# Filling the key and query stacks by way of DRAM, in a fused attention and gated-feed-forward kernel

## The chip, the cores and the metric

The kernel runs on one core of a Trainium2 chip. A core has five engines that run their own instruction streams: PE multiplies matrices (its weight loads, PEld, overlap the multiplications), DVE and ACT work element by element, POOL does the masks, and SP does nothing here but issue transfers (DMAs), in program order. The transfers are carried by 16 DMA engines, which all transfers share. The metric is the time of one execution on the device in microseconds (us), lower is better. Before the change the median of three runs is 737.2 us (735.12 to 738.53).

## The reference

One input `x` of 2048 tokens by 512 features goes through two branches, and a gate mixes them:

```python
qkv = x @ wqkv                      # 32 heads of 16
scores = einsum("bhqd,bhkd->bhqk", q, k) * 16 ** -0.5
mask = (i - j >= 0) & (i - j < 256) # each query sees itself and the 255 keys before it
a = (softmax(where(mask, scores, -1e9)) @ v) @ wo
b = (sigmoid(x @ w_gate) * (x @ w_up)) @ w_down    # 1376 hidden features
g = sigmoid((x * gate_w).sum(-1, keepdims=True))
out = g * a + (1 - g) * b
```

All inputs are fp32, and so is the result.

## The kernel before, in words

Precision: a product of two fp32 matrices is made as three products of split operands (high by high, high by low, low by high). A high part is a rounded copy made on ACT, the low part is the difference, made on DVE.

Attention: the 32 heads are taken in 8 groups of 4, a group's 2048 tokens in 16 blocks of 128. That makes 128 blocks `u` (NU); the main loop runs over them. For each block PE computes scores in both orientations: `s_part` (L324) gives queries by keys, of which DVE takes the row maximum (L330); `st_part` (L372), nine blocks later (LAG), gives keys by queries, of which ACT takes the exponential (L377). POOL masks the exponentials, and every fourth block `pv_part` (L407) multiplies them with the values. Between these pieces PE does the projections of later groups (`pj`, L252) and the gate and up products of the feed-forward branch (`gu`, L252); the list of turns is fixed in the program, and every engine but POOL keeps the written order. After the last block comes the down product (`pd`) and the output projection (`pa`).

Stacks: `s_part` and `st_part` do not read queries and keys as they were projected but as a *stack* of high and low parts, so that one multiplication over 64 rows gives the split product. A stack `t` holds 8 blocks (two projections `s`, 2t and 2t+1, of 512 columns each), and three of them lie in a ring (`ring`, RING = 3), so stack t takes the place of stack t-3. There are 16. The ring tile has 128 rows. In every group of four rows the rows 1, 2 and 3 hold feature values (high, low, high for keys or queries as the case may be), and row 0 is for constants and maxima. The path of a projection into the ring is: ACT copies it out of the accumulator (`pr`, L264); later ACT makes the high part `sh` (L275) and DVE the low part `sl` (L279), both 128 rows by 1024 columns once both halves are there; `stack_build` then issues one transfer that fills a constant row and twelve transfers of 32 rows by 4 KB that spread 32 rows of `sh` or `sl` over every fourth row of the ring (8 from `sh`, 4 from `sl`). They are issued from block u = 8t-7 on, four per block (SD); the stack is first read at block 8t.

Maxima: the softmax subtracts the row maximum inside the multiplication: the maximum of each query is a row of the stack. Every fourth block, the *visit*, `max_split` (DVE, L340 to L345) makes the negated maxima `nt` of four blocks; `max_store` (L348) writes them to DRAM (`max_scratch`), and `max_load` (L355, two transfers) reads them into row 0 of every 32 rows of the ring. `max_load` waits for its `max_store` to have landed. In a visit SP issues, in this order: `max_store`; four stores of the attention output `oT_scratch<-ob` and one of its sums (they wait for ACT's copy of the pv accumulator); `max_load`; and, in every second visit, the first stack transfers. `st_part` reads what `max_load` brought two blocks after the visit (where a visit opens a new group of heads, four blocks after).

Other traffic on SP: results of `gu` go to DRAM (`gu_scratch<-sp`), new weights come in (`guraw`, `wqraw`), and near the end four raw pieces of the last feed-forward columns (`tailraw`). The latter share two buffers with other weights; piece 2 can be loaded only after piece 0 has been split (`tail_split`, ACT then DVE, L534 and L535). `TAIL_LOAD` and `TAIL_SPLIT` give the block of each.

Each transfer signals one of eight semaphores in turn, and waits for the one eight places before it on SP.

Of the kernel before, what the change touches and what calls it, by code (L numbers as in the profile page):

```python
# [7 lines left out]
F32 = mybir.dt.float32  # L8
# [28 lines left out]
RING = 3  # L37
CH2 = 2 * CH
LAG = 9
PVLAG = LAG + 4  # L40
SD = 4
QB = 32
HOLD = 3
GAPS = [3] * 12 + [2] * 3
SHIFT = 6
TURN = ((0, 2, 1), (1, 0, 2))
TAIL_LOAD = {109: 0, 111: 1, 113: 2, 114: 3}
TAIL_SPLIT = {111: 0, 113: 1, 116: 2, 117: 3}
TREAD = 133
WD_LOAD = {124: 0, 125: 1, 126: 2, 127: 3, 128: 4, 129: 5, 130: 6, 131: 7, 132: 8, 133: 9, 135: 10}  # L50
WO = 125
# [6 lines left out]
def gated_mix_kernel(  # L58
# [11 lines left out]
    nc = tc.nc  # L70
# [22 lines left out]
    gu_d = nc.dram_tensor("gu_scratch", (2, NFM, P, T), F32, kind="Internal").ap()  # L93
    tail_d = nc.dram_tensor("tail_scratch", (NB, P, 2 * TF), F32, kind="Internal").ap()
    max_d = nc.dram_tensor("max_scratch", (NG * NC, P // QB, HG, 2, 4, QB), F32, kind="Internal").ap()
    fill_d = nc.dram_tensor("fill_scratch", (2, CH2), F32, kind="Internal").ap()

    cpool = ctx.enter_context(tc.tile_pool(name="cpool", bufs=1))
# [2 lines left out]
    ring = [ring_t[:, :, r * CH2:(r + 1) * CH2] for r in range(RING)]  # L101
# [34 lines left out]
    with ExitStack() as actx:  # L136
# [107 lines left out]
        pj = {}  # L244
        raws = {}
        parts = {}
        stg = {}

        def group_mm(pt, wh, wl, c, k, half, second):
            d, w = divmod(k, 2) if k < 2 * ND else (k - 2 * ND, 2)  # L250
            r = slice(0, P) if half is None else slice(64 * half, 64 * half + 64)
            return mm(pt, (wl if w == 2 else wh)[r, d], (xl if w == 1 else xh)[r, d, c * CH:(c + 1) * CH],  # L252
                      start=k == 0 and not second, stop=k == 3 * ND - 1 and (half is None or second),
                      skip_group_check=half is not None)
# [22 lines left out]
        def proj_lo(s):  # L277
            sh, sl = parts.pop(s)
            nc.vector.tensor_tensor(sl, pj.pop(s), sh.bitcast(F32), op=ALU.subtract)  # L279

        def stack_build(t):
            assert not {2 * t, 2 * t + 1} & {*pj, *parts}
            sh, sl = (v.bitcast(F32) for v in stg.pop(t))
            rt = ring[t % RING].bitcast(F32)
            st = rt.rearrange("(a r) j f -> r a j f", r=4)
            dmas = [fill_rows(t % RING, 0, 0)]
            if t < RING:
                dmas.append(fill_rows(t, 1, 1))
            for low in range(2):
                for j in range(4):  # L290
                    for r in range(3):
                        if low == (r == (1 if j < 2 else 2)):
                            dmas.append((st[r + 1, :, j], (sl if low else sh)[32 * j:32 * j + 32]))
            return dmas

        def run_dmas(dmas):
            for dst, src in dmas:
                nc.sync.dma_start(dst, src)  # L298
# [51 lines left out]
        def max_load(s):  # L350
            st = ring[s // 2 % RING].bitcast(F32).rearrange("(a r) j f -> r a j f", r=QB)
            o = s % 2 * CH
            src = max_d[s].rearrange("a (p s) l b t -> p (s l) b a t", p=2)
            for p in range(2):
                nc.sync.dma_start(  # L355
                    st[0, :, p, o:o + CH].rearrange("r (b a t) -> r b a t", b=4, a=P // QB), src[p],
                )
# [33 lines left out]
                    compare_op=ALU.is_gt, fill=0.0, base=0, channel_multiplier=1,  # L391
                )

        later = []
        acts = []
        evac = []
        exps = []
# [121 lines left out]
        def tail_load(d):  # L519
            raw_gu[d] = cpool.tile([P, D], F32, tag="wqraw", name=f"tailraw{d}", bufs=2)  # L520
            nc.sync.dma_start(raw_gu[d][:, 0:TW], wgu_tail[d])
# [97 lines left out]
        held = []  # L619

        def proj_group(s):
            return lambda k, h=None, x=False: proj_mm(s, k, h, x), lambda: None, lambda: proj_out(s)
# [148 lines left out]
        sdma = []  # L771
# [6 lines left out]
        for u in range(N):  # L778
# [9 lines left out]
                load_gu(0, 0)  # L788
                load_gu(0, 1)
            if u % 8 == 1 and u > 8 and u // 8 + 1 < NP:  # L790
                sdma = stack_build(u // 8 + 1)
            if u % 16 == 8 and u // 16 + 2 < NG:
                raw_q = load_wqk(u // 16 + 2)
            if u in (4, 8, NU):
# [25 lines left out]
            for s4 in proj_at.get(u, ()):  # L820
# [2 lines left out]
                        lambda k, h, s4=s4: proj_slot(s4, k, h), lambda s4=s4: proj_sum(s4)))  # L823
                else:
                    work.append(proj_group(s4))
            while held and u >= 8 * (held[0][0] // 2) - 10:
                acts.append(held.pop(0)[1])
            if u == N - 1:
                hold_group(*rest.pop(0))
# [74 lines left out]
        def blocks(v):  # L904
            return v.rearrange("p (d t) -> p d t", d=ND)
# [9 lines left out]
        rows = [blocks(free_slot(0, k, 3)) for k in range(2)]  # L915
# [32 lines left out]
        for n, (c, f) in enumerate(steps):  # L948
# [45 lines left out]
            for t in range(4):  # L994
                r = slice(t * QB, (t + 1) * QB)
# [67 lines left out]
```

## Time and profile before

| what | value |
|---|---|
| median of three runs | 737.2 us (735.12 to 738.53) |
| the profiled execution | 737.48 us, its span from first to last instruction 735.8 us |
| granted PE clock | 0.999 |
| busy share: PE, PEld, DVE, ACT, POOL | 99%, 80%, 66%, 58%, 23% |
| bytes moved by DMA | 103.64 MB, mean 141 GB/s |

How to read it: a row of the timeline gives the start in us, the length in us, the engine (SPq is SP issuing, not moving), the line, the operation, what is written and read, the shapes and a count; idle time before it and what ended it stand in brackets. A DMA's row on SPq is the time SP took to issue it; it lands later. A view by windows gives busy time per engine, the granted clock, the mean busy share of the 16 DMA engines, and GB/s. The view of DMA packets counts what the DMA engines carried in a window: each packet is one run of bytes, and the small packets include the 4-byte writes by which each DMA engine that took part in a transfer tells that its share has landed. A busy PE is not PE at its peak, since matmuls are pipelined and their ends are modelled.

### The profile page before, as it was taken

How to read it: one execution, taken by the hardware profiler on the slowest of the kernel's cores; microseconds unless marked ns; L12 is line 12 of the kernel's file. 1: busy time of each engine (PE TensorE's matmuls, PEld its weight loads, DVE VectorE, ACT ScalarE, POOL GpSimd, SP SyncE). 2: the span in 40 equal slices, each digit the busy share in tenths (PEclk: the TensorE clock that was granted, in tenths of full speed). 3: DMA queues.
4: the chain of work that ended last, by engine and by line, in shares of the span. 5: the costliest groups of instructions: out<-in, count | busy, mean ns of one | idle time of the engine just before them, and what ended most of it. 6: DMA issues, size and time to landing. Idle time of an engine off the chain costs nothing.

```text
span 735.8 us, 17513 instructions
## 1 busy us (share of the span) xinstructions
PE 724.9 (99%) x6298; PEld 591.0 (80%) x6298; DVE 488.4 (66%) x1455; ACT 423.5 (58%) x890; POOL 167.0 (23%) x255
## 2 busy tenths in 40 slices
PE   9999999999999999999999999999999999999997
PEld 7888788778887788787888777878888888888886
DVE  5368767666776676766677676666846787658481
ACT  6423666566676566656667655765667564534341
POOL 5200333232233233323223322232332000000000
PEclk9999999999999999999999999999999999999999
DMA  8441425344253442534525335362667997779431
GB/s 288 120 116 41 107 81 157 96 129 133 89 165 87 153 134 74 158 99 132 146 86 144 108 100 136 100 187 94 195 185 209 239 258 197 204 162 262 125 80 58
DMA packets 97039, 103.64 MB, mean 141 GB/s; under 512 B 47646, under 2 KB 60446, under 8 KB 96952
## 3 DMA queue, kind: packets, MB, share of 16 engines
q1 hardware_dynamic: 96808, 102.39, 49.8%
q8 instruction: 50, 0.82, 0.5%
q14 instruction: 37, 0.30, 0.1%
q10 hardware_dynamic: 144, 0.13, 0.1%
HBM read 45.32 MB, written 31.99 MB: 105 GB/s over the span
## 4 chain that ended last, share of the span: by engine, by line
PE 93%; DMA 2%; SPq 2%; issue 1%; DVE 1%; ACT 1%; DVEq 0%; ACTq 0%
PE gu L252 26%; PE pv L407 11%; PE pj L252 10%; PE s L324 6%; PE st L372 5%; PE tp L542 5%; PE pd L87 5%; PE pd L86 5%; PE pd L88 5%; PE vh L579 3%; PE pa L86 2%; PE pa L88 2%; PE pa L87 2%; SPq L298 2%; PE vps L445 2%
## 5 line engine op out<-in xcount | busy, mean ns | idle before, releaser
L330 DVE CUSTOM_DVE_ANT_0 junk<-s,mask 128x384 f32<-128x384 f32 (+2 forms) x512 | 272.0, 531 | 143.1 <-PE s L324 75.3
L377 ACT ACTIVATE pbuf<-st 128x384 f32<-128x384 f32 (+2 forms) x512 | 241.3, 477 | 166.6 <-PE st L372 110.7
L252 PE MATMUL gu<-xh,w 64*128 64x512 f32 x1152 | 282.4, 393 | 0.0
L252 PE MATMUL gu<-xl,w 64*128 64x512 f32 x576 | 186.8, 391 | 0.0
L372 PE MATMUL st<-ring 64*128 64x384 f32 (+2 forms) x536 | 167.7, 329 | 4.1 <-DMA ring<-max_scratch 2.8
L383 POOL TENSOR_SCALAR_AFFINE_SELECT pbuf<-pbuf 128x512 f32<-128x512 f32 x128 | 83.9, 655 | 376.0 <-ACT pbuf L377 334.9
L252 PEld LDWEIGHTS gu<-xh,w 64*128 64x128 f32 x1152 | 156.9, 185 | 11.6
L324 PE MATMUL s<-ring 64*128 64x384 f32 (+2 forms) x536 | 164.5, 325 | 1.0 <-DVE mx L330 0.6
L324 PEld LDWEIGHTS s<-ring 64*128 64x128 f32 x536 | 94.9, 184 | 22.5 <-DVE mx L330 7.2
L372 PEld LDWEIGHTS st<-ring 64*128 64x128 f32 x536 | 96.1, 184 | 11.9 <-ACT pbuf L377 2.3
L252 PEld LDWEIGHTS gu<-xl,w 64*128 64x128 f32 x576 | 90.5, 185 | 3.7
L407 PE MATMUL pv<-pbuf,V 128*32 128x384 f32 (+2 forms) x1408 | 84.3, 386 | 0.0
L252 PE MATMUL pj<-xl,wqh 64*128 64x512 f32 (+1 forms) x228 | 83.1, 392 | 0.0
L252 PE MATMUL pj<-xh,wqh 64*128 64x512 f32 (+1 forms) x228 | 83.0, 393 | 0.0
L407 PEld LDWEIGHTS pv<-pbuf,V 128*32 128x32 f32 x1408 | 41.4, 110 | 40.9 <-issue 30.5
L389 POOL TENSOR_SCALAR_AFFINE_SELECT pbuf<-pbuf 128x512 f32<-128x512 f32 x112 | 73.8, 659 | 0.0
L252 PE MATMUL pj<-xh,wql 64*128 64x512 f32 (+1 forms) x228 | 70.5, 393 | 0.0
L86 PE MATMUL pd<-ring,hb 128*128 128x512 f32 x160 | 62.3, 389 | 0.0
L88 PE MATMUL pd<-ring,hb 128*128 128x512 f32 x160 | 62.3, 389 | 0.0
L87 PE MATMUL pd<-ring,hb 128*128 128x512 f32 x160 | 62.2, 389 | 0.0
L82 ACT CAST hb<-V 128x512 fp32r<-128x512 f32 x40 | 24.9, 622 | 57.9 <-DVE V L743 44.8
L504 ACT COPY sp<-gu 128x512 f32<-128x512 f32 x72 | 42.2, 586 | 3.9 <-DMA gu_scratch<-sp 3.9
(127 smaller groups left out, 1108.9 us busy)
## 6 DMA issues: line engine op xcount, KB each, us to landing
gu_scratch<-sp SPq DMA_DIRECT2D x72, 256.0 KB
V<-gu_scratch SPq DMA_DIRECT2D x36, 512.0 KB
ring<-sh SPq DMA_DIRECT2D x128, 128.0 KB
ring<-sl SPq DMA_DIRECT2D x64, 128.0 KB
guraw<-in_wgu_dram SPq DMA_DIRECT2D x18, 256.0 KB
oT_scratch<-ob SPq DMA_DIRECT2D x128, 32.0 KB
xl<-oT_scratch SPq DMA_DIRECT2D x16, 256.0 KB
V<-in_xT_dram SPq DMA_DIRECT2D x15, 256.0 KB
```

Of the source, the lines that this page charges most:

```text
L86: mm(ps, lh, rh, start=first, stop=False)
L87: mm(ps, lh, rl, start=False, stop=False)
L88: mm(ps, ll, rh, start=False, stop=last)
L252: return mm(pt, (wl if w == 2 else wh)[r, d], (xl if w == 1 else xh)[r, d, c * CH:(c + 1) * CH], start=k == 0 and not second, stop=k == 3 ...
L324: mm(pt[:, (k - k0) * P:(e - k0) * P], lhsT, blk(g, k, hh, 1, e - k), start=k == k0, stop=e == i + 1, skip_group_check=True,)
L330: nc.vector.tensor_tensor_reduce(junk[:, 0:n], pt[:, 0:n], mask[:, 3 * P - n:], scale=1.0, scalar=NEG, op0=ALU.add, op1=ALU.max, accum_out ...
L372: mm(pt[:, (q - j) * P:(e - j) * P], lhsT, blk(g, q, hh, 0, e - q), start=q == j, stop=e == last, skip_group_check=True,)
L377: exps.append(nc.scalar.activation(p_blk(u, hh, 0, n), pt[:, 0:n * P].rearrange("p (b t) -> p b t", t=P), AF.Exp, scale=SCALE,))
L383: nc.gpsimd.affine_select(pbuf[:, s0], pbuf[:, s0], pattern=[[0, HG], [1, P]], compare_op=ALU.is_ge, fill=0.0, base=0, channel_multiplier=-1,)
L389: nc.gpsimd.affine_select(old, old, pattern=[[0, HG], [-1, P]], compare_op=ALU.is_gt, fill=0.0, base=0, channel_multiplier=1,)
L407: mm(pv[32 * hh:32 * hh + 32, (q - q0) * P:(e - q0) * P], Vf[:, v:v + 32], p_blk(g * NB + j, hh, q - j, e - q), start=j == j0, stop=j == q ...
L504: nc.scalar.copy(t, gp.pop((f, c, w)))
```

## The change

`sh` and `sl` of a stack are no longer spread from on-chip memory into the ring. As soon as the second half of `sl` is made, two stores (512 KB each) write them to a DRAM scratch of 4 by 2 by 32 by 1024 values per ring place; from block 8t-7 on, where the twelve transfers stood, five loads read them back into the ring (one of 512 KB, four of 256 KB), after the constant row's transfer, three per block (SD = 3). Stacks 0 and 1 are made as before; 14 are changed. To have the parts earlier, the making of `sh` and `sl` may begin at block 8t-13 instead of 8t-10. Two of the tail's raw pieces are loaded one block later, one a block earlier, and the first two are split earlier.

```diff
-SD = 4
+SD = 3
-TAIL_LOAD = {109: 0, 111: 1, 113: 2, 114: 3}
-TAIL_SPLIT = {111: 0, 113: 1, 116: 2, 117: 3}
+TAIL_LOAD = {109: 0, 110: 1, 114: 2, 115: 3}
+TAIL_SPLIT = {110: 0, 111: 1, 116: 2, 117: 3}
...
+    stack_d = nc.dram_tensor("stack_scratch", (RING, 4, 2, QB, CH2), F32, kind="Internal").ap()
...
         def proj_lo(s):
             sh, sl = parts.pop(s)
             nc.vector.tensor_tensor(sl, pj.pop(s), sh.bitcast(F32), op=ALU.subtract)
+            t = s // 2
+            made[t] = made.get(t, 0) + 1
+            if t > 1 and made[t] == 2:
+                for low, v in enumerate(stg.pop(t)):
+                    later.append((stack_d[t % RING, :, low], v.bitcast(F32)))
+
+        def stack_load(t):
+            assert made[t] == 2
+            rows = ring[t % RING].bitcast(F32).rearrange("(a r) j f -> r a j f", r=4)
+            dmas = [fill_rows(t % RING, 0, 0)]
+            if t < RING:
+                dmas.append(fill_rows(t, 1, 1))
+            for r, low, js in ((0, 0, (0, 4)), (1, 1, (0, 2)), (1, 0, (2, 4)), (2, 0, (0, 2)), (2, 1, (2, 4))):
+                js = slice(*js)
+                dmas.append((rows[r + 1, :, js], stack_d[t % RING, js, low].rearrange("j a f -> a j f")))
+            return dmas
...
             if u % 8 == 1 and u > 8 and u // 8 + 1 < NP:
-                sdma = stack_build(u // 8 + 1)
+                sdma = stack_load(u // 8 + 1)
...
-            while held and u >= 8 * (held[0][0] // 2) - 10:
+            while held and u >= 8 * (held[0][0] // 2) - 13:
                 acts.append(held.pop(0)[1])
```

PE's instructions keep their order entirely, and so do POOL's. On ACT and DVE only the makings of `sh` and `sl`, the splits beside them and the tail's first split move. SP's order changes at every stack. In the rows below, a shape stands behind each transfer (of what it writes), a count behind that, and an added list names the semaphores it waits for; after the change the program's line numbers are 17 higher there.

The first place is SP at stack 4, blocks 22 to 25. Before:

```order
121 L151 DMA wqraw_1850<-in_wqk_dram 128x512 [waits DMAHW1_49]
122 L298 DMA gu_scratch<-sp_3_1_1796 128x512 [waits DMAHW2_49,Activation_49]
123 L348 DMA max_scratch<-nt_1926 128x32 [waits DMAHW3_49,DVE_49]
124 L298 DMA oT_scratch<-ob_1937 16x512 [waits DMAHW4_49,Activation_49]
125 L298 DMA oT_scratch<-ob_1937 16x512 [waits DMAHW5_49]
126 L298 DMA oT_scratch<-ob_1937 16x512 [waits DMAHW6_49]
127 L298 DMA oT_scratch<-ob_1937 16x512 [waits DMAHW7_49]
128 L298 DMA sum_scratch<-ob_1937 4x512 [waits DMAHW0_49]
129 L355 DMA ring<-max_scratch 4x16x32 [waits DMAHW3_49,DMAHW1_49,PE_49]
130 L355 DMA ring<-max_scratch 4x16x32 [waits DMAHW2_49,PE_49]
131 L298 DMA ring<-fill_scratch 4x2x1024 [waits PE_49]
132 L298 DMA ring<-sh_1747 32x1024 [waits DMAHW4_49]
```

And now:

```order
111 L316 DMA gu_scratch<-sp_3_1_1786 128x512 [waits DMAHW0_49,Activation_49]
112 L316 DMA stack_scratch<-sh_1539 4x32x1024 [waits DMAHW1_49,Activation_49]
113 L316 DMA stack_scratch<-sl_1540 4x32x1024 [waits DMAHW2_49,DVE_49]
114 L366 DMA max_scratch<-nt_1918 128x32 [waits DMAHW3_49,DVE_49]
115 L316 DMA oT_scratch<-ob_1929 16x512 [waits DMAHW4_49,Activation_49]
116 L316 DMA oT_scratch<-ob_1929 16x512 [waits DMAHW5_49]
117 L316 DMA oT_scratch<-ob_1929 16x512 [waits DMAHW6_49]
118 L316 DMA oT_scratch<-ob_1929 16x512 [waits DMAHW7_49]
119 L316 DMA sum_scratch<-ob_1929 4x512 [waits DMAHW0_49]
120 L373 DMA ring<-max_scratch 4x16x32 [waits DMAHW3_49,DMAHW1_49,PE_49]
121 L373 DMA ring<-max_scratch 4x16x32 [waits DMAHW2_49,PE_49]
122 L316 DMA ring<-fill_scratch 4x2x1024 [waits PE_49]
```

The two stores stand right ahead of the visit's `max_store`, and the second of them waits for DVE's `sl`. It is so at stacks 4, 7, 10, 13 and 14. At stacks 3, 5, 6, 8, 9, 11 and 12 two to five transfers of `gu`, `guraw` and `wqraw` lie between, and at stack 15 the stores come right behind the loads of stack 14.

The second place is SP at stack 2, blocks 8 and 9. Before:

```order
25 L348 DMA max_scratch<-nt_804 128x32
26 L298 DMA ring<-fill_scratch 4x2x1024 x2
27 L298 DMA ring<-sh_448 32x1024 x2
28 L355 DMA ring<-max_scratch 4x16x32 x2
29 L298 DMA ring<-sh_448 32x1024 x6
30 L298 DMA ring<-sl_449 32x1024 x4
```

And now:

```order
25 L366 DMA max_scratch<-nt_804 128x32
26 L316 DMA stack_scratch<-sh_448 4x32x1024
27 L316 DMA stack_scratch<-sl_449 4x32x1024
28 L316 DMA ring<-fill_scratch 4x2x1024 x2
29 L316 DMA ring<-stack_scratch 32x4x1024
30 L373 DMA ring<-max_scratch 4x16x32 x2
31 L316 DMA ring<-stack_scratch 32x2x1024 x4
```

Here the `max_load` stands behind a load that needs the first store to have landed.

The third place is SP at blocks 113 to 115, in the tail. Before:

```order
268 L298 DMA gu_scratch<-sp_1_1_7720 128x512
269 L298 DMA gu_scratch<-sp_2_1_7748 128x512
270 L521 DMA tailraw_7820<-in_wgu_tail_dram 128x450
271 L298 DMA gu_scratch<-sp_3_1_7782 128x512
272 L348 DMA max_scratch<-nt_7849 128x32
273 L298 DMA oT_scratch<-ob_7860 16x512 x4
274 L298 DMA sum_scratch<-ob_7860 4x512
275 L355 DMA ring<-max_scratch 4x16x32 x2
276 L298 DMA ring<-fill_scratch 4x2x1024
277 L298 DMA ring<-sh_7658 32x1024 x7
278 L521 DMA tailraw_7931<-in_wgu_tail_dram 128x450
```

And now:

```order
287 L316 DMA gu_scratch<-sp_2_1_7689 128x512
288 L316 DMA gu_scratch<-sp_3_1_7723 128x512
289 L366 DMA max_scratch<-nt_7788 128x32
290 L316 DMA oT_scratch<-ob_7799 16x512 x4
291 L316 DMA sum_scratch<-ob_7799 4x512
292 L373 DMA ring<-max_scratch 4x16x32 x2
293 L316 DMA ring<-fill_scratch 4x2x1024
294 L316 DMA ring<-stack_scratch 32x4x1024
295 L316 DMA ring<-stack_scratch 32x2x1024 x4
296 L538 DMA tailraw_7868<-in_wgu_tail_dram 128x450
297 L316 DMA gu_scratch<-sp_0_0_7903 128x512
298 L538 DMA tailraw_7927<-in_wgu_tail_dram 128x450
```

The load of piece 2 stood ahead of a visit's `max_store` and stands behind the visit now; on DVE the split that it waits for (L535, `tail_wql`) moves ahead of eight row maxima.

More of the change, by code (lines that the diff above doesn't have):

```diff
@@ L247, in gated_mix_kernel @@
         stg = {}
+        made = {}
+        later = []
         def group_mm(pt, wh, wl, c, k, half, second):
@@ L279, in proj_lo @@
             nc.vector.tensor_tensor(sl, pj.pop(s), sh.bitcast(F32), op=ALU.subtract)
+            t = s // 2
[13 more added lines that the diff above has]
+            return dmas
         def stack_build(t):
-            assert not {2 * t, 2 * t + 1} & {*pj, *parts}
             sh, sl = (v.bitcast(F32) for v in stg.pop(t))
@@ L392, in mask_p @@
                 )
-        later = []
         acts = []
```

## The prediction, made before the result was known

> **What bounds the kernel now.** I read the page first, then PE's timeline for gaps, then SP's timeline around each gap.
>
> ```profile
> span 735.8 us, 17513 instructions
> PE 724.9 (99%) x6298; PEld 591.0 (80%) x6298; DVE 488.4 (66%) x1455; ACT 423.5 (58%) x890; POOL 167.0 (23%) x255
> PE 93%; DMA 2%; SPq 2%; issue 1%; DVE 1%; ACT 1%; DVEq 0%; ACTq 0%
> ```
>
> PE is the bound: it stands still for 10.9 us of 735.8, and 93% of the chain that ended last is PE. PE's program does not change, so there are only two ways to move the time: fill gaps of PE, or open new ones. The gaps of more than half a microsecond in the loop are these:
>
> ```profile
> 155.99 0.32 PE L372 MATMUL st<-ring 64*128 64x128 f32 x1 [1.09 <-DMA ring<-max_scratch]
> 459.96 0.44 PE L372 MATMUL st<-ring 64*128 64x384 f32 x1 [1.27 <-ACT pbuf L377]
> 483.07 0.42 PE L372 MATMUL st<-ring 64*128 64x384 f32 x1 [1.71 <-DMA ring<-max_scratch]
> 553.31 0.47 PE L542 MATMUL tp<-tail_wqh,xh 64*128 64x450 f32 x1 [0.69 <-ACT pbuf L377]
> ```
>
> Two of them wait for a `max_load`. SP shows why the first is late:
>
> ```profile
> 146.17 0.73 SPq L298 DMA_DIRECT2D ring<-sh  x1
> 146.96 2.54 SPq L298 DMA_DIRECT2D ring<-sl  x4
> 149.59 1.35 SPq L348 DMA_DIRECT2D max_scratch<-nt  x1
> 151.04 1.76 SPq L298 DMA_DIRECT2D oT_scratch<-ob  x4
> 152.85 0.55 SPq L298 DMA_DIRECT2D sum_scratch<-ob  x1
> 153.85 1.21 SPq L355 DMA_DIRECT2D ring<-max_scratch  x2
> ```
>
> SP is still issuing a stack's transfers, 0.6 us each, when `max_store` is due; the `max_load` behind it is issued at 153.85 and PE goes on at 155.99. A visit without a stack before it has SP free, and even there the time to spare is short:
>
> ```profile
> 223.86 0.32 SPq L348 DMA_DIRECT2D max_scratch<-nt  x1
> 227.26 1.71 SPq L298 DMA_DIRECT2D oT_scratch<-ob  x4
> 229.01 0.54 SPq L298 DMA_DIRECT2D sum_scratch<-ob  x1
> 229.66 1.14 SPq L355 DMA_DIRECT2D ring<-max_scratch  x2
> 232.67 0.33 PE L372 MATMUL st<-ring 64*128 64x384 f32 x1
> ```
>
> The last row is the first `st` product of the block that needs this load. From issue to PE's start it was 2.14 us at 155.99 (PE was waiting there), here 3.01: 0.9 us to spare. So every visit but the one in four that opens a group of heads runs with `max_load` about a microsecond ahead of PE. Whatever holds `max_load` back by more than that is paid in full. This is the place where the change decides.
>
> The gap at 483.07 has another origin:
>
> ```profile
> SPq L521 <- DVE mx L330: 8.3, 1, 8.3
> 467.10 2.06 SPq L298 DMA_DIRECT2D gu_scratch<-sp  x2
> 477.18 0.33 SPq L521 DMA_DIRECT2D tailraw<-in_wgu_tail_dram  x1
> ```
>
> SP stood 8 us at the load of tail piece 2, which waits for the split of piece 0, with a visit's `max_store` behind it.
>
> **The change part by part.**
>
> *Removed: SP's time.* Twelve transfers of about 0.6 us become five loads of the same kind and two stores. Some 3 us of SP per stack, 42 us over 14 stacks, lie beside PE and count only where a `max_store` is behind them: the gap at 155.99 (1.09 us) should close, and the one at 459.96 (1.27), where the chain runs through SP's stack transfers and the `gu` stores behind them. The tail's edit puts piece 2 behind the visit and splits piece 0 two blocks earlier: the gap at 483.07 (1.71) should close. Together 4.1 us of gain. The earlier making of `sh` and `sl` on ACT and DVE costs nothing: the same instructions three blocks earlier, on engines busy 58% and 66%; without that cover one of them is 0.7 us. The loads (1.5 MB as before) begin where the twelve transfers began, seven blocks before the stack is read; these hide them.
>
> *Added: two stores of 0.52 MB (128 rows of 4 KB each).* What they cost hangs on how many of the 16 DMA engines take part. Three windows of packets (around 230, 201 and 54.5 us) tell how many share a transfer here: `sum_scratch<-ob`, 4 rows; a `max_load` pair, 2 times 64 rows, with a fill of the ring beginning behind it; `max_store`, 128 rows.
>
> ```profile
> DMA packets 8, 0.01 MB, mean 8 GB/s; under 512 B 4, under 2 KB 4, under 8 KB 8
> DMA packets 141, 0.04 MB, mean 27 GB/s; under 512 B 136, under 2 KB 136, under 8 KB 140
> DMA packets 144, 0.02 MB, mean 11 GB/s; under 512 B 144, under 2 KB 144, under 8 KB 144
> ```
>
> Packets beyond the data are the engines' signs that they are done: 4 for the first; 136 - 128 = 8, so 4 each, for the `max_load`s; 144 - 128 = 16 for the last. The `max_load` is the telling one: its destination begins with a dimension of 4, its source with one of 16, its 64 rows could have gone over 16 engines, and they went over 4. The new stores have a destination 4x32x1024, beginning with 4 and not contiguous over it, and a source of 128 rows. The bounds are 4 engines, as with everything here that begins with a 4 on either side, and 16, since no row shows 4 beside 128 on-chip rows. I take 4.
>
> The Trainium skill says the same more generally (*DMA: Bandwidth & Descriptors*, section *Why a DMA increments its semaphore by 16 and not by 1*): the number of engines is the largest up to 16 that divides the slowest dimension of both sides, and those are the lowest-numbered ones. By it the stores get 4; the trace agrees for 4 with 4 and for 4 with 16, and no run here shows 4 with 128. The same page's *Rules for kernel authors* asks to join many small transfers into large ones, which would speak for the change; that is the first rival.
>
> How long four engines need for both stores:
>
> ```profile
> 8.00:12.00 4.00, 4.00 (x19) 3.24 (x18) 4.00 (x7) 3.71 (x7) 1.12 (x2) 1.00 1.05 394
> 139.00:149.00 10.00, 10.00 (x104) 8.07 (x102) 7.05 (x24) 5.79 (x14) 3.66 (x6) 1.00 0.80 220
> ```
>
> At best 394 GB/s over 16 engines, 24.6 each: 1.05 MB / 98.5 GB/s = 10.7 us. At the rate of the present stack phase, 220 GB/s at a busy share of 0.80, 17.2 each: 15.2 us. I take 11.5, near the first, as the stores have a queue of long rows and one side in DRAM like the transfers of that row.
>
> *The wait that it makes.* `max_store` uses all 16 engines, so its part on those four lies behind the stores, and `max_load` is not issued before it has landed. In an empty queue that takes 1.5 us:
>
> ```profile
> 53.60 0.33 SPq L348 DMA_DIRECT2D max_scratch<-nt  x1
> 55.07 1.26 SPq L355 DMA_DIRECT2D ring<-max_scratch  x2
> ```
>
> So `max_load` goes out at S + 13.0 (11.5 + 1.5), S being the stores' issue, and PE loses what that is beyond the usual time plus 0.9. S follows DVE's second `sl`, which keeps its place at stacks 4, 7, 10 and 13, where the stores stand right before `max_store`:
>
> ```profile
> 125.88 0.69 DVE L279 TENSOR_TENSOR sl<-pr,sh 128x512 fp32r<-128x512 f32 x1
> 137.65 1.19 SPq L355 DMA_DIRECT2D ring<-max_scratch  x2
> 220.20 0.69 DVE L279 TENSOR_TENSOR sl<-pr,sh 128x512 fp32r<-128x512 f32 x1
> 312.59 0.69 DVE L279 TENSOR_TENSOR sl<-pr,sh 128x512 fp32r<-128x512 f32 x1
> 322.59 1.13 SPq L355 DMA_DIRECT2D ring<-max_scratch  x2
> 406.15 0.72 DVE L279 TENSOR_TENSOR sl<-pr,sh 128x512 fp32r<-128x512 f32 x1
> 414.75 1.14 SPq L355 DMA_DIRECT2D ring<-max_scratch  x2
> ```
>
> With S 0.8 us after each `sl` start: 126.7 + 13.0 - 137.65 - 0.9 = 1.1; at 221.0, against the 229.66 above, 3.4; at 313.4, 2.9; at 407.0, 4.4. Together 11.8 us.
>
> Stack 2: the `max_load` stands behind a load that waits for the first store, and then queues behind the second on the same four engines.
>
> ```profile
> 67.70 0.33 SPq L348 DMA_DIRECT2D max_scratch<-nt  x1
> 77.73 0.49 ACT L377 ACTIVATE pbuf<-st 128x384 f32<-128x384 f32 x1 [0.37 <-PE st L372]
> ```
>
> Stores out at 68.1, load landed at 68.1 + 13.0 = 81.1; PE's product stands 0.4 before that exponential, at 77.3: 3.8 us. Stack 15:
>
> ```profile
> 446.85 0.50 SPq L298 DMA_DIRECT2D ring<-fill_scratch  x1
> 463.62 1.20 SPq L355 DMA_DIRECT2D ring<-max_scratch  x2
> ```
>
> The stores come behind the fill and the loads of stack 14, six issues of 0.6 us after 447.35, near 451; SP's usual `max_load` is at 463.62 there, about as late as S + 13.0; with PE no longer held at 459.96 I put 2.5.
>
> The other eight: the stores have up to nine microseconds more before the `max_load`. But each transfer waits for the one eight places before it, so that the `oT` stores may be held for the stack stores and issue behind them, 1.71 + 0.54 = 2.3 us. Between 0 and 2.3 each; I take 1.0, together 8.
>
> Sum: 11.8 + 3.8 + 2.5 + 8 - 4.1 = +22.0 us on the span, 757.8. Around the span the profiled execution has 737.48 - 735.8 = 1.7 us, and it lies 0.3 above the median of the runs, 737.2: **759 us**, 3.0% slower.
>
> **The rivals.**
>
> *Faster: the stores go over 16 engines.* Then they take 1.05 MB / 394 GB/s = 2.7 us, `max_load` could go at S + 4.2, everywhere before its usual time, and what is left is the 4.1 us of closed gaps: 733. For it: the source has 128 rows, and a transfer of 128 rows on both sides used 16. Against it: the `max_load`'s 64 rows. Chance 0.12; since 4.1 us is hardly above the bound of 0.5% (3.7 us, about what a measurement of this kernel can tell from no change), 0.09 of it faster, 0.03 the same.
>
> *Covered: the stores use four engines, but land ahead of need.* That would be so if `max_store` did not queue behind them, or if the slack were larger than 0.9 at most visits. At the four stacks above `max_load` would have to go 2 to 5 us later unpunished; the 1.09 us of 155.99 speaks against it. Losses of 4 us against gains of 4: 737. Chance 0.06, 0.05 of it the same, 0.01 slower.
>
> *Slower still: the drain takes 15.2 us.* Then all 13 exposed visits lose 3.7 us more: 759 + 48 = 807. This is the forecast's upper bound; chance 0.05 above 800.
>
> The forecast, with four engines and 8 to 13 visits late, has 0.77, on a range of its own of 746 (drain 10.7, the eight at nothing) to 800. Faster 0.09, same 0.08, slower 0.83. The range from 736 to 800 takes in the covered case and leaves out the faster one (0.12) and the far end.
>
> **What would show it.** Packets behind the two stores: 4 signs each, not 16, and a busy share near 0.25 for some 11 us. `max_load` issued 11 to 14 us after the stores where they stand before `max_store`. PE's waits on `ring<-max_scratch` up from 2.8 us in 2 to over 20 us in about 10, longest at stacks 2 and 13. No wait of 8 us on SP for the tail. If the share is near 1 for 3 us behind the stores, the four engines are wrong and with them the sum; if the share is 0.25 and PE doesn't wait, the slack is.

## The result and the profile after

The changed kernel takes 829.65 us (median of six runs, 825.47 to 831.66) against 736.95 us before (735.12 to 739.89, six runs beside them). The ratio is 1.124, with a 95% interval of 1.121 to 1.128. The prediction had the direction, but its 759 us and its range up to 800 us were both too low: the loss is 93 us, not 22.

The page of the kernel after, its head and the shares of the chain that ended last:

```profile
span 829.9 us, 17381 instructions
PE 757.0 (91%) x6298; PEld 625.1 (75%) x6298; DVE 488.0 (59%) x1455; ACT 425.0 (51%) x890; POOL 167.0 (20%) x255
PEclk9999899898989899898989898979999999999999
PE 74%; DMA 21%; DVE 3%; issue 1%; ACT 0%; SPq 0%; DVEq 0%; ACTq 0%
```

Two things have changed here, and they must be kept apart. PE stands still for 829.9 - 757.0 = 72.9 us, where it was 10.9 before: 62.0 us more. And PE's busy time has grown from 724.9 to 757.0, by 32.1 us, though its 6298 products are the same. The two make up the whole 94.1 us of span. The row PEclk shows where the second part comes from: the granted clock dips once for nearly every stack (0.942 in the mean, 0.999 before).

What PE waits for, and what SP waits for, in the views of waits (total us, times, longest):

```profile
PE st L390 <- DMA ring<-max_scratch: 65.4, 14, 10.4
...
SPq L373 <- DMA max_scratch<-nt: 30.0, 15, 4.9
SPq L316 <- DMA stack_scratch<-sl: 27.6, 9, 4.6
```

It was 2.8 us in two waits before. Fourteen stacks were changed, and there are fourteen gaps. PE's timeline shows them; here are those of stacks 2, 3, 4, 14 and 15:

```profile
85.91 0.65 PE L390 MATMUL st<-ring 64*128 64x384 f32 x1 [8.83 <-DMA ring<-max_scratch]
...
120.74 0.66 PE L390 MATMUL st<-ring 64*128 64x384 f32 x1 [2.64 <-DMA ring<-max_scratch]
158.97 0.66 PE L390 MATMUL st<-ring 64*128 64x384 f32 x1 [4.92 <-DMA ring<-max_scratch]
...
532.67 0.41 PE L390 MATMUL st<-ring 64*128 64x384 f32 x1 [1.21 <-DMA ring<-max_scratch]
558.48 0.66 PE L390 MATMUL st<-ring 64*128 64x384 f32 x1 [10.43 <-DMA ring<-max_scratch]
```

The nine others lie between 3.28 and 5.38 us. How one of them comes about is seen at stack 4. SP's timeline:

```profile
139.79 0.55 SPq L316 DMA_DIRECT2D stack_scratch<-sh  x1
140.92 0.53 SPq L316 DMA_DIRECT2D stack_scratch<-sl  x1
145.45 0.33 SPq L366 DMA_DIRECT2D max_scratch<-nt  x1
...
151.28 0.51 SPq L316 DMA_DIRECT2D sum_scratch<-ob  x1
156.73 1.18 SPq L373 DMA_DIRECT2D ring<-max_scratch  x2
```

And the chain of waits in the same place:

```profile
145.45 11.21 DMA max_scratch<-nt
...
156.73 2.10 DMA ring<-max_scratch
...
158.97 0.66 PE st L390
```

A `max_store` of 16 KB takes 11.21 us, because part of it lies behind the two stores; SP has issued everything else by 151.8 and stands until 156.73; PE stands until 158.97. This is the wait that the prediction described.

The stores do go over four engines. At stack 2 SP issues them at 67.55 and 68.18, and nothing else large moves until 78.85. The view by windows (us; busy time of PE, PEld, DVE, ACT and POOL; clock; DMA share; GB/s), and the packets from 75.0 to 75.7 and from 78.1 to 78.5, with the signs of the first store (between the two there is none):

```profile
69.00:74.00 5.00, 5.00 (x42) 4.16 (x38) 4.83 (x14) 3.75 (x8) 0.77 (x2) 1.00 0.25 52
74.00:79.00 5.00, 3.08 (x27) 2.32 (x25) 2.83 (x10) 1.48 (x3) 1.81 (x3) 1.00 0.26 102
```

```profile
DMA packets 17, 0.06 MB, mean 88 GB/s; under 512 B 2, under 2 KB 2, under 8 KB 17
DMA packets 11, 0.04 MB, mean 92 GB/s; under 512 B 2, under 2 KB 2, under 8 KB 11
```

The share is a quarter, 4 of 16 engines, for ten microseconds. Two signs come by 75.7 and two more only after 78.1: four engines, and two of them are later than the others by 2.4 us or more. In the first half the four move 52 GB/s, in the second 102. My 98.5 GB/s for four engines holds for the second half alone.

### The profile page after: what moved, and what is told of

Read it like the earlier page. It is cut to its first block, busy times and chain, and to the rows that moved or that the text cites. A ratio compares the mean times of both kernels' runs of the same rounds, so it can differ in the third digit from the quotient of the medians.

```text
span 829.9 us, 17381 instructions
## 1 busy us (share of the span) xinstructions
PE 757.0 (91%) x6298; PEld 625.1 (75%) x6298; DVE 488.0 (59%) x1455; ACT 425.0 (51%) x890; POOL 167.0 (20%) x255
## 4 chain that ended last, share of the span: by engine, by line
PE 74%; DMA 21%; DVE 3%; issue 1%; ACT 0%; SPq 0%; DVEq 0%; ACTq 0%
PE gu L255 20%; DMA max_scratch<-nt 14%; PE pj L255 8%; PE pv L424 6%; PE s L342 5%; PE st L390 5%; PE tp L559 5%; PE pd L88 4%; PE pd L86 4%; PE pd L87 4%; DMA ring<-max_scratch 4%; PE vh L596 2%; DVE junk L348 2%; PE pa L86 2%; PE pa L87 2%; PE pa L88 2%
## 5 line engine op out<-in xcount | busy, mean ns | idle before, releaser
L255 PE MATMUL gu<-xh,w 64*128 64x512 f32 x1152 | 299.0, 407 | 0.0
L390 PE MATMUL st<-ring 64*128 64x384 f32 (+2 forms) x536 | 177.5, 347 | 65.4 <-DMA ring<-max_scratch 65.4
L255 PE MATMUL gu<-xl,w 64*128 64x512 f32 x576 | 196.1, 406 | 0.0
L255 PEld LDWEIGHTS gu<-xh,w 64*128 64x128 f32 x1152 | 169.5, 194 | 9.8
L390 PEld LDWEIGHTS st<-ring 64*128 64x128 f32 x536 | 102.4, 196 | 75.7 <-issue 70.5
L342 PEld LDWEIGHTS s<-ring 64*128 64x128 f32 x536 | 100.2, 194 | 19.4 <-DVE mx L348 5.4
L255 PEld LDWEIGHTS gu<-xl,w 64*128 64x128 f32 x576 | 97.2, 195 | 3.5
L255 PE MATMUL pj<-xh,wqh 64*128 64x512 f32 (+1 forms) x228 | 95.2, 444 | 0.0
L255 PE MATMUL pj<-xl,wqh 64*128 64x512 f32 (+1 forms) x228 | 93.5, 436 | 0.0
L255 PE MATMUL pj<-xh,wql 64*128 64x512 f32 (+1 forms) x228 | 80.7, 442 | 0.0
L255 PEld LDWEIGHTS pj<-xh,wql 64*128 64x128 f32 (+1 forms) x228 | 48.8, 218 | 2.3
```

The costliest lines, as they stand in the source:

```text
L342: mm(pt[:, (k - k0) * P:(e - k0) * P], lhsT, blk(g, k, hh, 1, e - k), start=k == k0, stop=e == i + 1, skip_group_check=True,)
L390: mm(pt[:, (q - j) * P:(e - j) * P], lhsT, blk(g, q, hh, 0, e - q), start=q == j, stop=e == last, skip_group_check=True,)
```

## The experiments

Two theories stood against each other at first. **W** (width): the stores lie on 4 of 16 engines, what is queued behind them comes late, PE stands. **D** (detour): it is the way through DRAM itself, 14 MB more of traffic and loads that must await a landing. Beside them **C** asks whether PE's clock falls because of the gaps, and what that costs.

**The same change with stores over 16 engines.**

```diff
-    stack_d = nc.dram_tensor("stack_scratch", (RING, 4, 2, QB, CH2), F32, kind="Internal").ap()
+    stack_d = nc.dram_tensor("stack_scratch", (RING, 2, 4, QB, CH2), F32, kind="Internal").ap()
-                    later.append((stack_d[t % RING, :, low], v.bitcast(F32)))
+                    later.append((stack_d[t % RING, low].rearrange("j a f -> (j a) f"), v.bitcast(F32)))
-                dmas.append((rows[r + 1, :, js], stack_d[t % RING, js, low].rearrange("j a f -> a j f")))
+                dmas.append((rows[r + 1, :, js], stack_d[t % RING, low, js].rearrange("j a f -> a j f")))
```

> The scratch is laid out with `sh` and `sl` as its outer dimension, so that each store writes 128 contiguous rows; its loads, the order of SP and everything else are the change's. Theory W (the stores sit on 4 of 16 engines, `max_store` and `max_load` behind them come late, PE stands and its clock drops): 16 signs per store, a DMA share near 1 for some 3 us behind the stores in place of 0.25 for 11 to 16, no PE wait on ring<-max_scratch above 1 us, clock 0.99 or more, 731 to 737 us. Theory D (it is the way through DRAM, its 14 MB more of traffic and the loads that must await a landing, whatever the width): the waits of 14 stacks stay at least half as long, 60 us in all become 30 or more, and the time is 790 to 830 us.

Measured: 732.58 us, 0.993 of before (0.990 to 0.995). The busy times on its page, PE's wait for the maxima, and the windows behind the stores of stack 2:

```profile
PE 722.5 (99%) x6298; PEld 589.7 (81%) x6298; DVE 487.3 (67%) x1455; ACT 423.5 (58%) x890; POOL 167.1 (23%) x255
```

```profile
PE st L390 <- DMA ring<-max_scratch: 0.2, 1, 0.2
```

```profile
68.00:70.00 2.00, 2.00 (x22) 1.87 (x19) 1.86 (x6) 0.05 (x1) 0.00 (x0) 1.00 0.81 315
70.00:72.00 2.00, 2.00 (x17) 1.80 (x15) 1.86 (x8) 1.93 (x5) 0.00 (x0) 1.00 0.67 250
```

W holds, D falls: with the same bytes, the same order on SP and loads of the same sizes, all fourteen gaps and the dips of the clock are gone, and the kernel is 0.7% faster than before. One thing beside the width changes here: a store now writes one contiguous block. The run with 8 engines below separates the two. The order of a DRAM tensor's dimensions was worth 97 us.

**Half the dose.** The `sh` store goes to a scratch of its own in 128 contiguous rows, `sl` stays as it was.

```diff
+    high_d = nc.dram_tensor("high_scratch", (RING, 4, QB, CH2), F32, kind="Internal").ap()
-                    later.append((stack_d[t % RING, :, low], v.bitcast(F32)))
+                    later.append((stack_d[t % RING, :, low] if low else high_d[t % RING].rearrange("j a f -> (j a) f"), v.bitcast(F32)))
...
```

> Half the dose: the `sh` store goes to a scratch of its own in 128 contiguous rows, the `sl` store stays as in the change, so one 0.52 MB store lies on 4 engines instead of two. W: that store alone takes 5.6 us (my 98.5 GB/s) to 8 us (half of the 15.6 us that the two take at stack 4 in the profile after), `max_load` comes 6 to 8 us earlier than after the change; of the 14 gaps of 1.2 to 10.4 us all but those at stacks 2 and 15 (8.83 and 10.43) are gone, and these are below 4: 734 to 750 us. If the loss were linear in the bytes on 4 engines: half of 93, some 783 us. D: no difference from the change, 820 to 832 us.

Measured: 751.56 us, 1.020 (1.016 to 1.025). PE's gaps of over half a microsecond that wait for the maxima:

```profile
82.05 0.66 PE L391 MATMUL st<-ring 64*128 64x384 f32 x1 [4.75 <-DMA ring<-max_scratch]
...
476.54 0.66 PE L391 MATMUL st<-ring 64*128 64x384 f32 x1 [5.19 <-DMA ring<-max_scratch]
```

Only stacks 2 and 15 are left, as W said, with gaps of 5 us where it had said below 4; the time is 1.6 us above W's range. The loss is a threshold and not a slope: half of the bytes on four engines cost a sixth of the loss (2.0% of 12.4%). At the twelve other stacks the narrow store cost next to nothing: the largest gap there that waits for the maxima is 0.49 us, so the store must have drained before it held `max_load` back.

**A width between: 8 engines.** The scratch's outer dimension is 8; a load may not step over the new dimension, so five loads become ten, issued five per block in place of three (SD = 5).

```diff
-    stack_d = nc.dram_tensor("stack_scratch", (RING, 4, 2, QB, CH2), F32, kind="Internal").ap()
+    stack_d = nc.dram_tensor("stack_scratch", (RING, 8, 2, QB // 2, CH2), F32, kind="Internal").ap()
...
+                src = stack_d[t % RING, 2 * js.start:2 * js.stop, low].rearrange("(j b) a f -> b a j f", b=2)
+                for b in range(2):
+                    dmas.append((rows[r + 1, 16 * b:16 * b + 16, js], src[b]))
```

> A dose between the change (4 engines) and the 16-engine layout: the scratch's outer dimension is 8, each store writes 8x16x1024, and the five loads become ten of 16 rows, since a load may not step over the new dimension (SP issues eleven rows per stack as against thirteen in the kernel before). The drain decides (W): with 8 signs per store and 8 engines, 256 / 8 x 0.159 = 5.1 us if the packets go at 159 ns from the start, 8 us if they begin as slowly as on 4 engines (the first 20 of each engine at 291 ns). In the half dose the pair took some 10 us and only stacks 2 and 15 stalled, for 9.9 us together, 751.6 us in all; so here PE waits on ring<-max_scratch below 5 us and 732 to 742 us. If the loss came from anything else that the 16-engine layout also changed (one contiguous block per store), not from the number of engines: waits as in the change, 800 us or more.

Measured: 753.23 us, 1.022 (1.019 to 1.026). The wait for the maxima, and two windows behind the stores of stack 2:

```profile
PE st L392 <- DMA ring<-max_scratch: 13.4, 4, 6.6
```

```profile
69.00:73.00 4.00, 4.00 (x34) 3.53 (x32) 3.85 (x12) 2.48 (x6) 0.00 (x0) 1.00 0.46 91
73.00:77.00 4.00, 4.00 (x37) 3.18 (x36) 3.42 (x13) 2.34 (x6) 1.35 (x2) 1.00 0.54 183
```

The share is a half, and the slow first half is there again, 91 and then 183 GB/s. The number of engines orders the times: 733, 753 and 830 us with 16, 8 and 4. The rival of the contiguous block falls: a store is as scattered here as in the change, and yet PE waits 13.4 us for the maxima and not 65.4. My 732 to 742 was too low: I had taken the waits below 5 us, and they are 13.4, of which 11.6 again at stacks 2 and 15. But the 753 us are not the width's alone, since the ten loads change SP's order too. At stack 2 `max_load` now stands behind three loads, and the third needs the second store, not only the first. The chain of waits there:

```profile
68.87 10.97 DMA stack_scratch<-sl
...
80.53 2.02 DMA ring<-max_scratch
```

At stack 15 five more loads stand ahead of the two stores; `max_store` goes out late, at 472.89, and lands in 4.36 us. How much of the two stalls is the loads' was not measured.

**Why the four engines start slowly: distance of their addresses?** In the change the four engines of a store write 256 KB apart. Here one unused row is put behind each place.

```diff
-    stack_d = nc.dram_tensor("stack_scratch", (RING, 4, 2, QB, CH2), F32, kind="Internal").ap()
+    stack_d = nc.dram_tensor("stack_scratch", (RING, 4, 2 * QB + 1, CH2), F32, kind="Internal").ap()
-                    later.append((stack_d[t % RING, :, low], v.bitcast(F32)))
+                    later.append((stack_d[t % RING, :, low * QB:(low + 1) * QB], v.bitcast(F32)))
...
```

> The change with one unused row of 4 KB behind the 64 rows of each of the scratch's four outer places, so that the four engines of a store no longer write at a distance of 256 KB from each other but of 260 KB. Bytes, packets, engines (4) and all orders stay. In the profile after, the first half of each store pair runs at 47 to 53 GB/s and the packets end in step (four at a time, 291 ns each), the rest at 100 GB/s (159 ns). Theory A (the four engines hold each other up because their addresses lie 256 KB apart): the packets take 159 ns from the start, the pair drains in 256 / 4 x 0.159 = 10.2 us, `max_load` comes 4 to 5 us earlier, the PE waits fall from 65.4 to 20 us or less, and the time is 750 to 770 us, where I had forecast it with a drain of 11.5. Rival B (a store over 4 engines starts slowly for some other cause, such as the side it reads): no change, 822 to 832 us.

Measured: 829.42 us, 1.124 (1.120 to 1.128). The windows at stack 2, which comes 0.6 us later here:

```profile
70.00:75.00 5.00, 5.00 (x42) 4.23 (x40) 4.71 (x15) 3.75 (x8) 1.18 (x2) 1.00 0.26 58
75.00:80.00 5.00, 2.68 (x25) 2.00 (x21) 2.54 (x10) 1.48 (x3) 1.39 (x3) 1.00 0.25 100
```

Theory A falls: the same slow half, the same time. What slows the first half stays open. It is there with 4 and with 8 engines and not with 16. That it is the side of the stores that reads on-chip memory was not tried.

**PE kept awake in the wait.** Filler products of `xh` by `xh` are put in front of the waiting product of the 14 blocks, into the accumulator that it then overwrites. All transfers and waits stay.

```diff
+FILL = {4 * s - 2: 18 for s in range(3, 25, 2)} | {2: 50, 98: 6, 102: 60}
...
+            if hh == 1:
+                for _ in range(FILL.get(u, 0)):
+                    mm(pt[:, 0:3 * P], xh[:, 0, 0:P], xh[:, 0, 0:3 * P], start=True, stop=True, skip_group_check=True)
```

> The change, with filler products (128x384, into the accumulator of `st`, which the real product then overwrites) in the 14 blocks where PE waits for `max_load`: 18 at most of them, 50, 6 and 60 at stacks 2, 14 and 15, so that PE is at work in the first part of the wait or all of it. All DMAs and waits stay. Theory C (of the 94 us of span, some 32 are PE's own clock, which falls to 0.50 after each gap of 2.6 us or more): granted clock 0.98 or more, gaps before `st` below 2 us, PE busy up only by the filler (282 products of about 0.17 us at full clock, 50 us or so, in place of the idle 62), and 797 to 806 us. If the drop of the clock is not caused by the gaps (or PE's longer products are a mere way of counting): 825 us or more.

Measured: 808.4 us, 1.095 (1.091 to 1.099); the granted clock is 1.000 in the mean. From its page, and the group of the filler among PE's instructions (busy us, mean ns, idle before):

```profile
PE 784.2 (98%) x6612; PEld 652.8 (81%) x6612; DVE 488.3 (61%) x1455; ACT 423.7 (53%) x890; POOL 167.1 (21%) x255
...
L392 PE MATMUL st<-xh 128*128 128x384 f32 x314 | 58.4, 340 | 0.0
```

More work on PE made the kernel 21 us faster. PE's busy time without the filler is 784.2 - 58.4 = 725.8, that of the kernel before (724.9): the 32 us of longer products are gone, so they were the clock's, and the clock fell because PE stood. Filler and idle time together, 58.4 + 18.6 = 77.0 us, are 4 us more than the change's 72.9 of idle time, so the filler ran a little over, and 21 us (27 between the two profiled executions) is a lower bound of what the clock costs. 808.4 lies 2.4 us above the range that I had given, which counted on 282 filler products where there are 314. Two gaps, of 2.12 and 2.48 us, stayed above the 2 us that I had expected, and the clock did not fall behind them.

**The tail tables alone**, in the kernel before.

```diff
-TAIL_LOAD = {109: 0, 111: 1, 113: 2, 114: 3}
-TAIL_SPLIT = {111: 0, 113: 1, 116: 2, 117: 3}
+TAIL_LOAD = {109: 0, 110: 1, 114: 2, 115: 3}
+TAIL_SPLIT = {110: 0, 111: 1, 116: 2, 117: 3}
```

> The kernel before with the change's two tail tables alone. My step: the 8.3 us wait of SP in the tail goes and with it the gap of 1.71 us at 483.07: 735.3 us, 0.2% less. Rival (the tail edit moves the gap to a later place: split 0 now stands ahead of eight row maxima on DVE): 737 us or more, with a new gap between 470 and 550 us.

Measured: 735.0 us, 0.997 (0.995 to 0.999). PE's largest gap from 440 us on:

```profile
552.37 0.47 PE L542 MATMUL tp<-tail_wqh,xh 64*128 64x450 f32 x1 [2.99 <-ACT pbuf L377]
```

The gap of 1.71 us at 483.07 is gone, and the one before `tp` has grown from 0.69 to 2.99 us. So both had a part: the median of twelve runs is the 735 that I had expected (the profiled execution, at 738.12, lies above it), and in this execution a gap did move to a later place.

**The 16-engine layout with the old tail tables.**

> The 16-engine layout with the two tail tables as before the change. It took 732.6 us with the new tables, and the tail tables alone gave 2.4 us to 3.0 us at the kernel before. If the two gains add up: 735 to 736 us, with the gap near 480 us and SP's wait of 8 us back. If the way through DRAM gives all of it by itself: 732.6 as with the new tables.

Measured: 737.47 us, 1.000 (0.998 to 1.002), above both values that I had named: the stacks' way gives nothing that can be told without the new tail tables. SP's wait for the split of tail piece 0 and PE's gaps:

```profile
SPq L538 <- DVE mx L348: 8.4, 1, 8.4
```

```profile
479.87 0.41 PE L390 MATMUL st<-ring 64*128 64x384 f32 x1 [2.26 <-DMA ring<-max_scratch]
...
553.73 0.47 PE L559 MATMUL tp<-tail_wqh,xh 64*128 64x450 f32 x1 [1.86 <-ACT pbuf L395]
```

The gaps of 1.09 and 1.27 us that the stack transfers had made are closed, but those in the tail are larger than before (2.26 for 1.71, 1.86 for 0.69). In the wide layout the tail tables bring 4.9 us (737.5 to 732.6), in the kernel before 3.0 (738.05 to 735.0). The likely reading is that what the stacks save ahead of the tail is waited for in it unless the tail is mended too; the stacks' own share on top of the tables, some 2 us, is at the edge of what the intervals (0.990 to 0.995 and 0.995 to 0.999) tell apart.

**The 16-engine layout with the parts made later** (8t-10 in place of 8t-13).

> The 16-engine layout with the making of `sh` and `sl` begun at block 8t-10 as before the change. With stores that drain in 3 us, an earlier beginning buys nothing: 732 to 734 us, and the PE wait on ring<-max_scratch stays under 1.5 us. Rival Q (the earlier beginning is what keeps the loads on time, as their source must have landed first): gaps before `s` products that wait for ring<-stack_scratch, or `max_load` held by the loads, and 736 us or more.

Measured: 733.51 us, 0.995 (0.993 to 0.997), and its only gap above 0.6 us in the loop is one of 2.26 us before `tp`. The earlier beginning buys nothing that can be told.

**The earlier beginning alone**, in the kernel before.

```diff
-            while held and u >= 8 * (held[0][0] // 2) - 10:
+            while held and u >= 8 * (held[0][0] // 2) - 13:
```

> The kernel before with `sh` and `sl` made from block 8t-13 on, nothing else changed. My step: it costs nothing and gains nothing, 736 to 739 us. If the earlier makings crowd ACT and DVE at the visits: new gaps before `st` products, 740 us or more.

Measured: 792.74 us, 1.076 (1.073 to 1.079). This was a surprise. What DVE and PE wait for:

```profile
DVE sl L279 <- DMA ring<-sl: 48.1, 7, 10.4
```

```profile
PE s L324 <- DVE mx L330: 22.8, 9, 5.9
```

`sl` of the next stack is made into the buffer that the twelve transfers of the last one are still reading; DVE, in its written order, stands up to 10.4 us in front of it with the row maxima behind, and PE waits for these. PE waits 18.7 us more for exponentials of ACT, which stands for the same transfers in front of `sh`, and its busy time grows to 739.6 us at a granted clock of 0.968, so part of this loss is the clock's too. The stores of the change free the buffer sooner (no wait of DVE or ACT for them is left in its profile), and there the earlier beginning does no harm (the wide layout with it took 732.6 us, without it 733.5).

## Why the prediction was right in kind and wrong in size

The mechanism was the predicted one in each of its steps: PE bounds the kernel, `max_load` runs about a microsecond ahead of it, the stores use four engines, `max_store` has a share on these and lands late, PE waits. What failed are sizes, and one term that was not there. Either fault alone would have left the time inside the range that ends at 800, the first barely: the stalls as measured without the clock come to 737.2 + 62.0 = 799 us, the forecast's stalls with the clock's part to 759 + 32 = 791. The forecast's sum against the two profiled executions:

| term of the sum | forecast, us | measured, us |
|---|---|---|
| stacks 4, 7, 10, 13 | 11.8 | 4.92 + 5.38 + 4.68 + 5.02 = 20.0 |
| stack 2 | 3.8 | 8.83 |
| stack 15 | 2.5 | 10.43 |
| "the other eight" | 8 | 26.2 |
| gaps closed | -4.1 | -3.4 |
| PE's clock behind the gaps | no term | 32.1 |
| sum | +22.0 | +94.1 |

*The removed work.* The closed gaps are 2.8 us of waits for the maxima, which are counted anew in the lines above, and 0.6 of the rest (8.1 us of other idle time before, 7.5 after). That they close was right, and SP's wait of 8 us in the tail is gone; that this is a gain by itself held for the tail tables alone (735.0 us), not for the stacks alone (737.47 in the wide layout with the old tables).

*"Costs nothing."* The prediction let the earlier making of `sh` and `sl` cost nothing because ACT and DVE have time to spare. That it cost nothing in the change was luck: alone it cost 56 us, since not the engines' time decides but when the buffer comes free, and the stores happen to free it sooner.

*Four engines.* Right, by the signs and the share. The Trainium skill's rule for the number of engines (*DMA: Bandwidth & Descriptors*, *Why a DMA increments its semaphore by 16 and not by 1*), the largest number up to 16 that divides the slowest dimension of both sides, gives 4, 8 and 16 for the three layouts. The trace agrees: four signs in the rows above, and in the windows in which the signs of the first store come, with 16 engines (69.75 to 70.00 us) and with 8 (72.9 to 74.9):

```profile
DMA packets 41, 0.10 MB, mean 410 GB/s; under 512 B 16, under 2 KB 16, under 8 KB 41
```

```profile
DMA packets 89, 0.33 MB, mean 166 GB/s; under 512 B 8, under 2 KB 8, under 8 KB 89
```

*"I take 11.5, near the first."* This is the first step that failed. I chose between 10.7 us (the best rate of a full queue) and 15.2 us (the rate of the stack phase) and took the wrong end. At stacks 4, 7, 10 and 13 `max_load` was issued 15.1 to 15.8 us behind the second store, where the prediction had S + 13.0; taking off the 1.5 us of `max_store`, the drain is by this estimate 13.6 to 14.3 us behind that store's issue, and 14.6 to 15.4 behind the first one's. Four engines that start at 52 GB/s are not a quarter of sixteen at full rate, and no row before showed four engines under load. With S + 15.4 the four stacks would have come out at 11.8 + 4 x 2.4 = 21.4 us; 20.0 was measured.

*"Between 0 and 2.3 each; I take 1.0."* This failed next, and through the same number. The eight stacks whose stores have a lead lost 1.21 to 4.48 us each. At stack 5, SP's timeline shows both parts of it:

```profile
177.40 0.53 SPq L316 DMA_DIRECT2D stack_scratch<-sl  x1
...
183.87 0.59 SPq L366 DMA_DIRECT2D max_scratch<-nt  x1
186.62 5.71 SPq L316 DMA_DIRECT2D oT_scratch<-ob  x4
...
194.21 1.16 SPq L373 DMA_DIRECT2D ring<-max_scratch  x2
```

The lead of the second store over `max_store` is 6.5 us here, not the nine that I allowed; the `oT` stores take 5.71 us to issue because one of them waits for a stack store eight places before, as the prediction said, but `max_load` goes 16.8 us behind the second store, not at 13. At the eight stacks the lead is 6.5 to 8.5 us. With 5.8 us from `max_store` to `max_load` (223.86 to 229.66 before) and 0.9 to spare, a lead of 6.5 covers a drain of 11.5 and the 1.5 of `max_store`, but not a drain of 14.

*Stack 2 and stack 15.* At stack 2 the prediction had the load landed at 81.1. The chain after shows it issued at 79.60, right behind the first load of the stack, and landing at 85.78:

```profile
67.55 11.28 DMA stack_scratch<-sh
...
79.60 6.18 DMA ring<-max_scratch
```

The first store alone took 11.28 us, and what was left of the second one lay ahead of `max_load` on its four engines; I had named that queue and given it no price of its own. At stack 15 `max_load` went 19.4 us behind the second store (536.89 to 556.29); I had put 2.5 us there from a likeness, without a row that showed the load. The longest waits are at stacks 15 and 2, and not at 2 and 13.

*The missing term.* The prediction counted a stall as the time that PE stands. Here each stall of 2.64 us or more was also followed by a stretch at half the clock. The windows around the gaps of 2.64 us (120.74) and 4.92 us (158.97) in the kernel after, and around one of 1.21 us (532.67):

```profile
120.00:124.00 4.00, 3.26 (x18) 3.29 (x20) 0.57 (x2) 1.90 (x4) 0.00 (x0) 0.57 0.71 215
124.00:128.00 4.00, 4.00 (x42) 3.69 (x42) 3.35 (x11) 2.94 (x7) 1.23 (x2) 1.00 0.98 342
...
160.00:164.00 4.00, 4.00 (x24) 4.00 (x22) 1.13 (x4) 1.14 (x3) 0.00 (x0) 0.50 1.01 350
...
532.00:536.00 4.00, 3.33 (x31) 3.36 (x32) 2.08 (x8) 2.88 (x7) 0.53 (x1) 1.00 0.59 166
```

PE runs 24 products in four microseconds at 0.50 and 42 at 1.00. With thirteen such stretches this is 32.1 us of longer products, a third of the loss; keeping PE awake took at least 21 us of it back. The gaps of the kernel before, up to 1.71 us, left the clock at 1.00 and so gave no hint of it. The Trainium skill states such a gate (*TensorE: Matmul & The Clock Gate*, *Part 1: The HAM clock gate*): half the clock after an idle window of some 3.4 us, and full clock again after as long at work. The trace agrees on the half and on the kind, while shorter gaps were enough here (2.64 us, and less in other runs, see the last section). The prediction should have weighed that rule against its own stalls of up to 4.4 us.

*The rivals.* "Slower still" (a drain of 15.2 us, 807 us) was the nearest and had 0.05 of the chance; without the clock's part the change would have come to the 799 us above, so the stalls that this rival gave were nearly right in sum (48 us more than forecast, 39 measured), though spread otherwise. The rival with 16 engines said 733 us, and the layout that gives 16 engines took 732.6; the size was right, but in part by luck: the tail tables alone gave 735.0, the stacks alone nothing, and only both together 732.6.

*What the range left out.* It was bounded by the drain alone. Eight terms that all hang on one number were added as if a mean of 1.0 were safe, and no case let several be wrong together.

## What to carry to other kernels

Before a transfer through DRAM is costed by its bytes, look at the outer dimension of both sides: here 4, 8 and 128 gave 4, 8 and 16 engines. A small transfer on all engines that is queued behind a narrow one can wait for it to the end (11.21 us here, 1.5 in an empty queue). Where a stall of a few microseconds is predicted on PE, allow for a stretch at half the clock behind it (2.5 us for each of thirteen stalls here), and treat the stalls of one repeated pattern as one number that is right or wrong everywhere. An edit that seems to cost nothing beside another (the earlier beginning) may rest on it: alone it cost 56 us.

## What was not expected of the hardware

- Stores over 4 and over 8 engines began at half their later rate: 52 and then 102 GB/s on four, 91 and then 183 on eight, for about 5 and 4 us. Two of the four engines sent the sign of the first store by 75.7 us and two after 78.1. Over 16 engines the same rows ran at 315 GB/s from the first window on. Setting the addresses 260 in place of 256 KB apart changed nothing; the cause is open.
- The length of a gap does not alone decide whether the clock falls. A gap of 2.64 us halved it (120.00:124.00 above), and one of 2.52 us, `st` at 533.51 us in the kernel with the padded scratch, left it at 1.00:

```profile
533.51 0.41 PE L390 MATMUL st<-ring 64*128 64x384 f32 x1 [2.52 <-DMA ring<-max_scratch]
```

```profile
533.00:537.00 4.00, 3.49 (x32) 3.52 (x34) 2.17 (x6) 3.04 (x7) 0.00 (x0) 1.00 0.62 169
```

But the gap of 2.26 us in the wide layout with the old tail tables (`st` at 479.87 above) was followed by half the clock, 1.5 us after PE had resumed:

```profile
482.00:484.00 2.00, 2.00 (x13) 2.00 (x12) 0.57 (x2) 0.97 (x2) 0.00 (x0) 0.50 0.99 365
```

So was one of 1.81 us in the kernel with the earlier beginning alone (`s` at 164.77; 0.56 from 167 to 170 us), while one of 2.34 us in the same execution (`st` at 535.40) left the clock at 1.00. These are single gaps of single executions; what decides beside the length is open.
